# DeltaNet with a multiplicative FFN on one core: corner products of the inverses on four parts of the array, and a new order of all steps

## The chip, the cores and the metric

The kernel runs on one core of a Trainium2 chip. The metric is the device time of one execution in microseconds (us). The profile is one further execution, taken by the hardware profiler; its span is that from the first to the last instruction. In its views PE is TensorE's matmul, PEld its weight load, DVE VectorE, ACT ScalarE, POOL GpSimd and SP SyncE; a q behind a name (SPq) is the engine's queue of instructions, where it issues DMAs. L473 is line 473 of the kernel.

## What is computed

A delta-rule attention over 4 batches, 8 heads, 768 steps and head size 48 feeds a feed-forward block of 3072 tokens, model width 384 and inner width 1024, all in fp32:

```python
k_n = k / (np.linalg.norm(k, axis=-1, keepdims=True) + 1e-06)
for t in range(S):
    kt, vt, bt = (k_n[:, :, t], v[:, :, t], beta[:, :, t, None])
    y[:, :, t] = np.einsum('bhd,bhde->bhe', q[:, :, t], state)
    v_old = np.einsum('bhde,bhd->bhe', state, kt)
    state = state + bt[:, :, :, None] * np.einsum('bhd,bhe->bhde', kt, vt - v_old)
...
a = x @ w1
b = x @ w2
h = a * b @ w3
return (h @ w_out).astype(np.float32)
```

## The kernel before

**Chunks and inverses.** The sequence is cut into 12 chunks of 64 steps (`C`), taken for all 32 pairs of batch and head at once: partitions 0 to 63 hold batches 0 and 1, partitions 64 to 127 batches 2 and 3 (`z` in the code). Within a chunk the recurrence needs the inverse of a triangular 64x64 matrix per pair. `scores` multiplies keys with keys and queries (`KQ`, L360 and L366) and leaves the triangular matrices in `U` and the query scores in `PT`. The inverse is made of 32x32 blocks. `to_blocks` (L408) writes the diagonal blocks of two chunks to DRAM (`Ud`), so that they come back with one block per partition (`Ub`, L420). `inverse` (the 31 steps of L434 and L439 on VectorE) inverts all of them; for the first two pairs of chunks it works in a two-bank PSUM buffer that it holds for that time. The result goes through DRAM (`Vd`, L447), and `from_blocks` (L452) puts the inverted blocks on the diagonal of `TT`, with four DMAs per chunk. `corner` then makes the off-diagonal block in two products per pair: VectorE transposes the upper blocks into `T11` (L464); the block of `U` beside the diagonal times `T11` (L473, 32 small matmuls) goes from quarter 2z of the partitions to quarter 2z+1; ScalarE copies it (L480); times the lower diagonal block (L487, 32 more) it comes back to quarter 2z; ScalarE writes it, negated, into `TT` (L494). Each such matmul has 32 rows, 32 weight columns and 32 moving columns, and its results go to the single-bank buffer `ps_t`.

**The recurrence and its output.** `chain` carries the state: state times keys (S,KQ), subtracted from v into `R`; `R` times `TT` into `X`; `X` times keys into the next state `S` (all L517, 32 matmuls each on 64-row parts of the array). `outputs` (L618) adds state times queries and `X` times `PT`; ScalarE copies it into `xT` (L639), and after every second chunk six DMAs (L650) bring 16 rows of each head group to where the FFN wants them.

**The FFN.** Weights come in pieces: a DMA into one of five `raw` buffers (L663), three ScalarE operations (L671 to L673), one on VectorE (L675) and two on GpSimd (L677, L678) make fp32 of what the inputs hold. `transpose_w3` (L713) and `fold` (L722) multiply w3 with w_out once, into `w34`. For every 128 steps of all four batches `ab` (L742) makes x @ w1 and x @ w2 in eight parts, with their elementwise product (L756), and `o` (L762) multiplies it with `w34`, copies it (L768) and writes it out (L771). These are full 128x128 matmuls of 384 or 512 columns; below they are called dense.

**Order.** Every part of the work is a Python generator that stops at each `yield`. `ORDER` names the part whose next step is written down; a letter for the kind and a number for the chunk or pair of chunks (K, Q, d: keys and queries by features; k, q, v, p: loads; g, N: norms; s: scores; u: to_blocks; V: inverse; e: corner; c: chain; y: outputs; P: a weight piece; t, f: fold; a, o: FFN). `in_text_order` then ties each engine to exactly that order:

```python
for name in ORDER.split():
    step(name)
in_text_order()
```

**PSUM and shared buffers.** `two_banks()` gives `psW` buffers of two banks in turn, two of them; `bank()` single banks of `psF`, three of them; `psT` is one bank. `in_turn` hands out named buffers one after the other, so that the n-th use waits for the end of the one that had the buffer before.

Of the kernel before, what the change touches and what calls it, by code (L numbers as in the profile page):

```python
# [37 lines left out]
P7 k0 g0 q0 V0 K0 g0 g0 k1 K0 K0 P7 P7 P7 K0 K0 Q0 Q0 Q0 Q0 Q0 g0 g0 g0 g0 K1 P0 P0 P0 P0 g0  # L38
P3 K1 K1 K1 P3 P3 s0 g0 beta beta g0 P1 P1 q1 P1 beta N0 s0 K1 Q1 Q1 Q1 P10 P3 s0 s0 Q1 Q1
P1 p2 s0 s0 s0 P10 P10 P10 P6 P6 s1 s1 s1 P11 s1 s1 s1 P6 P6 P13 N0 u0 u1 P11 P11 P12 P2 s1  # L40
d2 d2 t2 t2 P13 P13 N0 P11 P13 V0 V0 P2 P2 P23 V0 P12 P12 t5 P12 P2 P22 P23 P4 V0 P22 V0 V0
V0 V0 V0 P22 V0 V0 V0 t5 V0 P23 P4 P4 t3 t3 k3 t4 P22 t4 t14 t14 f2 P23 f1 P4 V0 V0 V0 V0 P5
P5 P5 v0 P20 P20 V0 V0 V0 V0 V0 t15 P5 f2 V0 V0 P21 P21 f1 f2 P20 n0 n0 f7 V0 V0 V0 V0 P21
V0 V0 V0 P15 P15 P15 V0 f1 V0 V0 t15 p3 P14 P14 s0 P20 k2 t12 f7 P17 t12 P14 f7 P21 t13 g1
g1 P15 f6 p2 d2 d2 g1 V0 V0 V0 t7 t13 d3 t7 P17 f6 f6 P14 g1 g1 g1 P18 t6 t6 P18 s2 e0 P17
g1 g1 f3 e0 g1 g1 N1 e0 P16 e0 P18 P16 s2 s2 s2 e1 e1 s2 s2 e0 f3 P16 e0 c0 c0 P9 P19 P19
P19 f3 P9 P9 P17 t9 t9 p3 P18 t10 t10 v1 y0 y0 e1 e1 P16 t8 t8 d3 d3 P8 d3 s3 s3 s3 P9 P8
P26 P26 s3 s3 s3 u2 P24 t1 t1 u3 c0 c0 P19 t11 P8 n1 n1 N1 N1 P24 e1 P25 V1 P26 P26 c1 f5
P24 c1 e1 c1 c1 t11 V1 V1 V1 V1 V1 V1 V1 V1 V1 V1 f5 f5 P8 t0 t0 k4 s1 y1 y1 V1 P31 V1 V1
P25 P25 f4 P24 V1 P30 V1 V1 V1 V1 V1 V1 f0 P25 P30 P31 P30 P32 g2 v2 P31 c1 P31 V1 V1 f0 V1  # L50
V1 f4 P28 f4 P30 P32 P32 P32 P28 f0 V1 V1 V1 V1 V1 y1 a01 p4 P28 a03 a01 k5 a00 a00 V1 V1
a03 P28 p4 a01 d4 V1 V1 V1 g2 g2 a01 c1 g2 g2 g2 g2 V1 V1 P27 P27 P27 P27 a00 a00 P29 a03
a03 V1 g2 d4 d4 P29 P29 P29 d4 e2 e2 a02 a02 a02 a02 g2 c2 e2 e2 P33 P33 a06 g2 N2 s4 a06 n2
n2 c2 e2 s4 e2 s4 a04 a04 c2 c2 P35 P35 P35 e3 P33 P33 a07 P34 P34 P34 P34 c2 c2 y2 a07 a05
p5 p5 d5 d5 d5 s4 s4 u4 s4 v3 P35 a06 y2 e3 e3 d5 a06 s5 s5 s5 s5 s5 s5 u5 a04 a04 a05 a05
a05 n3 n3 c3 c3 N2 N2 e3 e3 e3 a07 c3 a07 o03 V2 V2 V2 p6 V2 V2 V2 V2 o03 v4 o03 c3 y3 y3 V2
V2 V2 V2 V2 V2 V2 V2 V2 V2 V2 V2 c3 n4 k6 g3 V2 V2 V2 V2 o00 o00 y3 o01 o01 o01 a10 a10 a17
a17 g3 g3 a12 V2 v5 V2 V2 V2 p6 a12 a12 V2 V2 V2 V2 o02 V2 V2 V2 c3 c4 e4 e4 e4 a12 e4 a17
a17 o00 d6 d6 o02 o02 g3 n4 c4 e4 e4 a10 a10 c4 k7 g3 a11 c4 c4 c4 a13 a13 a15 a15 a11 y4 n5
e5 e5 e5 e5 a14 c5 a14 p7 d6 d6 p7 d7 g3 d7 d7 g3 g3 g3 e5 a16 y4 n5 c5 g3 s6 N3 s6 s6 d7 s6  # L60
s6 s6 a16 a16 s7 s7 V3 s7 s7 s7 u6 u7 a11 a11 s7 V3 e5 c5 a16 a13 a13 p8 c5 a14 a14 c5 a15
a15 y5 y5 V3 V3 V3 V3 V3 o12 o12 o13 V3 V3 V3 c5 V3 V3 V3 V3 V3 V3 k8 V3 V3 o13 V3 V3 y5 a20
a20 V3 V3 V3 d8 a27 a27 a23 a24 a24 k9 a23 a23 v6 n6 n6 V3 V3 V3 V3 V3 v7 V3 V3 a23 V3 o12
V3 V3 g4 g4 g4 g4 V3 V4 g4 g4 a27 a27 a20 o13 e6 e6 o10 o10 p8 o10 o11 o11 o11 d8 d8 e7 a20
e6 d8 N3 N3 c6 g4 g4 g4 g4 n7 n7 c6 e6 e6 a25 N4 s8 e7 s8 s8 a24 a24 s8 s8 s8 e6 c6 c6 p9 p9
a25 a25 a25 y6 y6 c6 c6 a21 e7 c7 a21 c7 u8 a22 e7 e7 a22 d9 d9 d9 d9 s9 a22 a22 s9 s9 s9 s9
s9 a21 a21 k10 e7 c7 c7 a26 y7 a26 p10 a26 a26 u9 V4 V4 V4 c7 o21 o21 y7 y7 V4 V4 V4 V4 V4
V4 V4 o22 o21 v8 V4 V4 o22 o22 V4 V4 V4 V4 V4 d10 o23 o23 v9 a35 a35 k11 a37 a37 V4 V4 V4 V4
V4 V4 V4 V4 a34 V4 V4 g5 V4 V4 a34 a37 V4 V4 V4 a35 a35 g5 g5 c7 a37 o20 o20 g5 g5 g5 V4 e9
e8 a36 e8 e8 e8 n9 g5 g5 g5 N4 N4 a36 c8 p10 d10 d10 n8 n8 c8 e8 e8 a30 v11 a30 g5 c8 a30 c8  # L70
y8 y8 d10 s10 a34 p11 p11 c8 e9 e9 a30 N5 n11 d11 d11 a34 d11 s10 s10 a32 d11 s11 s11 s11 V5
a32 a31 c8 a31 a31 a31 e9 e9 c9 n9 c9 s11 s11 s11 a36 n11 s10 s10 s10 u10 u11 V5 a32 a32 e9
c9 c9 a33 a36 a33 o23 a33 N5 y9 y9 y9 a33 o33 o33 o33 V5 V5 V5 o20 V5 V5 V5 o32 V5 V5 o32
o32 V5 V5 V5 N5 a40 a40 a40 V5 a43 V5 V5 V5 V5 V5 V5 V5 V5 V5 V5 a40 a41 a41 a41 a43 V5 V5
o31 a44 a44 o31 V5 a41 o30 v10 V5 c9 V5 V5 V5 o30 V5 V5 V5 e10 e10 o31 n10 n10 e10 a42 e10
e10 e10 e11 a42 c9 c10 a46 a46 a46 a46 c10 a42 a42 c10 c10 a47 a47 y10 y10 e11 e11 e11 a43
a43 c10 c10 o30 a45 a45 a45 a45 a47 a47 c11 c11 e11 e11 a44 a44 c11 c11 o40 o40 y11 o40 y11
y11 o42 o42 o42 o43 o43 o43 a57 a57 a57 a57 a56 a56 a52 a52 a53 a53 a50 a50 o41 a50 a52 a52
o41 o41 a50 a56 a56 a51 a51 a55 a53 a55 a53 a54 a54 a54 a54 a55 a55 a51 a51 o53 o53 o53 o51
o51 o51 o52 o52 o50 o50 o50 o52  # L80
# [4 lines left out]
def kernel(  # L85
# [14 lines left out]
    P = 128  # L100
# [19 lines left out]
    psT = ctx.enter_context(tc.tile_pool(name="psT", bufs=1, space=bass.MemoryType.PSUM))  # L120
    psF = ctx.enter_context(tc.tile_pool(name="psF", bufs=3, space=bass.MemoryType.PSUM))
# [23 lines left out]
    def bank(shape):  # L145
        return in_turn(psF, shape, "f", 3, "ps_f")
# [21 lines left out]
    strict = work.tile([P, P], FP32, name="strict", bufs=1)  # L168
# [10 lines left out]
    def padded(name, shape, n):  # L179
        res = []  # L180
        for i in range(n):
            t = persist.tile(shape, FP32, name=f"{name}{i}")
            pool.memset(t[:], 0.0)
            res.append(t)
        return res
# [5 lines left out]
    ktoks, vtoks, KQs, PTs, Us, Xs, Ss = {}, {}, {}, {}, {}, {}, {}  # L191
# [68 lines left out]
    def squares(j):  # L260
        sums[j] = ss = in_turn(small, [P, 2, 2, NR, H], "ss", 1, "ss")
        for cc in range(2):
            kt = ktoks[2 * j + cc]
            for r in range(NR):
                sq = in_turn(work, [P, H, D], "sq", 1, "sq")
                pool.tensor_tensor(out=sq[:], in0=kt[:, r], in1=kt[:, r], op=ALU.mult)  # L266
                yield
                dve.tensor_reduce(out=ss[:, 1, cc, r], in_=sq[:], axis=AX.X, op=ALU.add)  # L268
                yield
        yield from across(ss[:, 1], ss[:, 0])  # L270
# [79 lines left out]

    def scores(m):
        for r in range(NR):
# [18 lines left out]
            if r == 0:  # L371
                Us[m] = in_turn(work, [P, NR, H, C], "U", 2, "U")
            psv = ps[:].rearrange("p e (a j t) -> p a e j t", a=NP, j=2)
            dve.tensor_tensor(
                out=by_parity(Us[m][:, r]), in0=psv[:, :, :, 0, :],
# [27 lines left out]
    def to_blocks(m):  # L403
        j = m // 2
        if m % 2 == 0:
            Uds[j] = in_turn(dram, [P, BS, BS], "Ud", 2, "Ud")
        for x in range(4):
            sync.dma_start(  # L408
                out=Uds[j][:].rearrange(blocks, x=4, r=NR, h=H)[m % 2, x],
                in_=Us[m][quarter(x), :, :, quarter(x % 2)].rearrange("s r h t -> s (r h) t"),  # L410
            )
        yield
# [36 lines left out]

    def from_blocks(m):  # L450
        for x in range(4):
            sync.dma_start(  # L452
                out=TTs[m % 2][quarter(x), :, :, quarter(x % 2)].rearrange("s r h t -> s (r h) t"),
                in_=Vds[m // 2][:].rearrange(blocks, x=4, r=NR, h=H)[m % 2, x],
            )
        yield


    def corner(m):
        yield from from_blocks(m)  # L460
        TT = TTs[m % 2]

        X1 = T11 = in_turn(work, [P, NR, H, BS], "T11", 2, "T11")
        dve.transpose(  # L464
            out=T11[:].rearrange("p r h t -> p (r h) t"),
# [3 lines left out]
        ps = in_turn(psT, [P, NR, H, BS], "t", 1, "ps_t")  # L469
        for r in range(NR):  # L470
            for h in range(H):
                for z in range(2):
                    pe.matmul(  # L473
                        ps[quarter(2 * z + 1), r, h, :], lhsT=Us[m][quarter(2 * z), r, h, BS:C],
                        rhs=T11[quarter(2 * z), r, h, :], start=True, stop=True,
                    )
        yield
        for z in range(2):
            x = quarter(2 * z + 1)
            act.copy(out=X1[x], in_=ps[x])  # L480
        yield
        ps = in_turn(psT, [P, NR, H, BS], "t", 1, "ps_t")
        for r in range(NR):
            for h in range(H):
                for z in range(2):
                    x = quarter(2 * z + 1)
                    pe.matmul(  # L487
                        ps[quarter(2 * z), r, h, :], lhsT=X1[x, r, h, :],
                        rhs=TT[x, r, h, BS:C], start=True, stop=True,
                    )  # L490
        yield
        for z in range(2):
            x = quarter(2 * z)
            act.mul(out=TT[x, :, :, BS:C], in_=ps[x], mul=-1.0)  # L494
# [391 lines left out]
```

## Time and profile before

| | |
|---|---|
| time, median of 3 runs | 611.39 us (611.18 to 611.51) |
| span of the profiled execution | 610.1 us |
| mean granted TensorE clock | 0.991 |
| TensorE busy | 567.9 us |
| dense products: x @ w1, x @ w2, output, fold | 131.1, 131.5, 127.1, 46.8 us busy |
| corner products, first and second | 15.1, 14.6 us busy, 768 rows each |
| scores, both lines | 30.6 and 31.3 us busy |
| ScalarE copies of the first corner product | 24, 577 ns each |

A program matmul shows as two rows in these views, so 24 corner products of 32 matmuls are 1536 rows. A row lasts longer than the step from one row to the next[...]: what a phase costs is read from the start of one phase to the start of the next, in the timeline. A line of the timeline gives the start, the length, engine, line, operation, output and inputs, shapes and the number of rows run together; what stands in brackets is idle time before it. In a line of busy times by stretches there follow, after the stretch and its length, PE, PEld, DVE, ACT and POOL with the number of instructions, then the granted clock, the DMA engines' share and GB/s.

### The profile page before, as it was taken

How to read it: one execution, taken by the hardware profiler on the slowest of the kernel's cores; microseconds unless marked ns; L12 is line 12 of the kernel's file. 1: busy time of each engine (PE TensorE's matmuls, PEld its weight loads, DVE VectorE, ACT ScalarE, POOL GpSimd, SP SyncE). 2: the span in 40 equal slices, each digit the busy share in tenths (PEclk: the TensorE clock that was granted, in tenths of full speed). 3: DMA queues.
4: the chain of work that ended last, by engine and by line, in shares of the span. 5: the costliest groups of instructions: out<-in, count | busy, mean ns of one | idle time of the engine just before them, and what ended most of it. 6: DMA issues, size and time to landing. Idle time of an engine off the chain costs nothing.

```text
span 610.1 us, 17982 instructions
## 1 busy us (share of the span) xinstructions
PE 567.9 (93%) x7804; PEld 333.7 (55%) x7804; DVE 322.0 (53%) x752; ACT 183.2 (30%) x373; POOL 145.3 (24%) x150
## 2 busy tenths in 40 slices
PE   3736988999899999999999999999999999999997
PEld 2724667644565655655466655465564655644454
DVE  1569875697665955557946449556386123100110
ACT  2776667654530212402111302122121212211100
POOL 6489866575242101100130000112001000000000
PEclk9999997899999999999999999999999999999999
DMA  9668887867755255253356324551321300000001
GB/s 216 163 207 195 195 176 168 193 118 155 158 77 105 67 116 85 30 94 72 62 119 87 55 55 96 101 74 23 57 81 26 97 2 2 24 30 13 1 13 39
DMA packets 202223, 55.67 MB, mean 91 GB/s; under 512 B 192352, under 2 KB 195424, under 8 KB 202144
## 3 DMA queue, kind: packets, MB, share of 16 engines
q1 hardware_dynamic: 197952, 53.74, 42.0%
q10 hardware_dynamic: 4192, 0.79, 0.9%
q8 instruction: 61, 1.00, 0.7%
q14 instruction: 18, 0.15, 0.1%
HBM read 42.30 MB, written 11.01 MB: 87 GB/s over the span
## 4 chain that ended last, share of the span: by engine, by line
PE 83%; SPq 5%; DMA 4%; ACT 3%; DVE 2%; issue 1%; POOL 1%; ACTq 0%; POOLq 0%; DVEq 0%
PE ps_f L742 38%; PE ps_f L762 20%; PE ps_f L722 5%; PE ps_w L517 5%; PE ps_w L618 4%; PE ps_t L473 2%; PE ps_w L366 2%; PE ps_t L487 2%; PE ps_w L360 2%; SPq L226 2%; PE ps_f L713 1%; SPq L663 1%; DMA X<-in_q_dram 1%; DMA raw<-in_moe_w_out_dram 1%; DMA ktok<-in_k_dram 1%
## 5 line engine op out<-in xcount | busy, mean ns | idle before, releaser
L742 PE MATMUL ps_f<-xT,w1s 128*128 128x512 f32 x288 | 131.1, 600 | 1.5 <-DMA xT<-xT 1.5
L742 PE MATMUL ps_f<-xT,w2s 128*128 128x512 f32 x288 | 131.5, 600 | 0.5 <-DVE ab L756 0.5
L762 PE MATMUL ps_f<-w,ab 128*128 128x384 f32 x384 | 127.1, 488 | 0.1
L756 DVE TENSOR_TENSOR ab<-a,ps_f 128x512 f32<-128x512 f32 x48 | 32.6, 683 | 136.5 <-PE ps_f L742 135.6
L762 PEld LDWEIGHTS ps_f<-w,ab 128*128 128x128 f32 x384 | 72.3, 190 | 51.5 <-issue 3.3
L742 PEld LDWEIGHTS ps_f<-xT,w2s 128*128 128x128 f32 x288 | 53.0, 190 | 61.2 <-issue 57.6
L742 PEld LDWEIGHTS ps_f<-xT,w1s 128*128 128x128 f32 x288 | 53.0, 190 | 60.4 <-issue 55.0
L751 ACT COPY a<-ps_f 128x512 f32<-128x512 f32 x48 | 27.7, 585 | 148.3 <-PE ps_f L742 116.5
L266 POOL TENSOR_TENSOR sq<-ktok 128x384 f32<-128x384 f32 x24 | 20.2, 844 | 147.7 <-DVE ss L268 82.1
L768 ACT COPY osb<-ps_f 128x384 f32<-128x384 f32 x24 | 11.5, 479 | 126.0 <-PE ps_f L762 97.0
L503 POOL TENSOR_TENSOR vtok<-vtok,n 128x384 f32<-128x384 f32 x24 | 20.2, 858 | 117.0 <-DMA vtok<-in_v_dram 103.9
L439 DVE TENSOR_TENSOR Vb<-Vb,tb 128x31 f32<-128x31 f32 (+15 forms) x124 | 45.2, 364 | 4.3
L722 PE MATMUL ps_f<-w2s,w3T 128*128 128x384 f32 x128 | 46.8, 518 | 0.1
L434 DVE TENSOR_TENSOR tb<-Vb,Ub 128x31 f32<-128x31 f32 (+15 forms) x124 | 43.9, 354 | 4.6 <-DMA Ub<-Ud 0.7
L639 ACT COPY xT<-ps_w 48x256 f32<-48x256 f32 x96 | 30.5, 366 | 48.4 <-PE ps_w L618 31.9
L722 PEld LDWEIGHTS ps_f<-w2s,w3T 128*128 128x128 f32 x128 | 24.9, 202 | 16.3 <-issue 2.7
L366 PE MATMUL ps_w<-KQ 48*64 48x64 f32 x768 | 31.3, 241 | 0.0
L360 PE MATMUL ps_w<-KQ 48*64 48x128 f32 x384 | 30.6, 307 | 0.7 <-ACT PT L386 0.7
L360 PEld LDWEIGHTS ps_w<-KQ 48*64 48x64 f32 x384 | 25.3, 154 | 8.6 <-issue 6.6
L713 PE MATMUL ps_f<-ident,w 128*128 128x128 f32 x64 | 12.6, 335 | 17.9 <-POOL w L678 17.9
L366 PEld LDWEIGHTS ps_w<-KQ 48*64 48x64 f32 x768 | 28.7, 154 | 0.3 <-issue 0.2
L581 DVE TENSOR_TENSOR S<-S,ps_w 48x768 f32<-48x768 f32 x20 | 19.0, 950 | 9.7 <-PE ps_w L517 9.5
(94 smaller groups left out, 642.4 us busy)
## 6 DMA issues: line engine op xcount, KB each, us to landing
raw<-in_moe_w_dram SPq DMA_DIRECT2D x16, 512.0 KB, 5.5
vtok<-in_v_dram SPq DMA_DIRECT2D x24, 192.0 KB, 4.0
raw<-in_moe_w_dram SPq DMA_DIRECT2D x24, 192.0 KB, 4.2
out_dram<-osb SPq DMA_DIRECT2D x24, 192.0 KB, 2.0
ktok<-in_k_dram SPq DMA_DIRECT2D x44, 96.0 KB, 3.4
raw<-in_moe_w_out_dram SPq DMA_DIRECT2D x8, 384.0 KB, 4.8
Ud<-U SPq DMA_DIRECT2D x48, 64.0 KB, 2.0
Ub<-Ud SPq DMA_DIRECT2D x6, 512.0 KB, 3.4
```

The costliest lines, as they stand in the source:

```text
L360: pe.matmul(ps[half(z), 0, n : n + 128], lhsT=x[:, 0, :], rhs=x.rearrange("p j t -> p (j t)"), start=True, stop=True,)
L366: pe.matmul(ps[half(z ^ j), 1, n + C * j : n + C * j + C], lhsT=x[:, 0, :], rhs=x[:, j, :], start=True, stop=True,)
L434: dve.tensor_tensor(out=tv, in0=V[:, 0 : s + 1, s : s + 1].to_broadcast([P, s + 1, n]), in1=U[:, s, s + 1 : BS].unsqueeze(1).to_broadcast( ...
L439: dve.tensor_tensor(out=o, in0=o, in1=tv, op=ALU.subtract)
L517: pe.matmul(out(ps, r, h, z), lhsT=lhs(r, h, z), rhs=rhs(r, h, z), start=True, stop=True,)
L618: i = pe.matmul(region(h, z, r), lhsT=lhs, rhs=rhs, start=part[n] not in part[:n], stop=part[n] not in part[n + 1 :],)
L639: act.copy(out=xT[f, p:NP:2, b : b + NR, cc, :].rearrange("p a r t -> p r a t"), in_=pyv[f, z, b : b + NR],)
L722: pe.matmul(ps[:, 0:DM], lhsT=w3Ts[jc, kc // 4][:, kc % 4 * P : kc % 4 * P + P], rhs=wo[:, kc], start=(kc == 0), stop=(kc == KF - 1),)
L742: pe.matmul(ps[:], lhsT=w[:, m, js], rhs=x[:, m].rearrange("p b c t -> p (b c t)"), start=(m == 0), stop=(m == KM - 1),)
L751: act.copy(out=a[:], in_=ps[:])
L756: dve.tensor_tensor(out=t[:], in0=a[:], in1=ps[:], op=ALU.mult)
L762: pe.matmul(ps[:, 0:DM], lhsT=abs_[u, jc][:, b * P : (b + 1) * P], rhs=w34[:, jc, :], start=(jc == 0), stop=(jc == KF - 1),)
```

## The change

- **Corner products.** Both products use 64-row, 64-column parts of the array: rows 64z to 64z+32 (33 rows, the last of them zeros in one operand), 33 weight columns, 33 output partitions. The output goes to the half z of even heads and to the other half of odd heads, so that all four parts are used; the two parities go to the two banks of a `psW` buffer. The second product, of heads that crossed over, takes them back. It reads the lower diagonal block from a new tile `T22`, which holds odd heads on the other half.
- **`from_blocks`** loads `T22` with four more DMAs per chunk (eight in place of four).
- **Buffers.** `U` and `T11` are persistent tiles with 8 more columns that are set to zero; `T11` is one buffer in place of two; `T22` is two. `psT` is gone and `psF` has four banks. `strict` and the squares `sq` share the buffers of the output copies (`o`).
- **`ORDER`** is written anew from the first step to the last: the same steps but in another sequence on all engines. Weight pieces begin with P0 in place of P7; corners, chains and scores stand at other places among the dense products.

```diff
-P7 k0 g0 q0 V0 K0 g0 g0 k1 K0 K0 P7 P7 P7 K0 K0 Q0 Q0 Q0 Q0 Q0 g0 g0 g0 g0 K1 P0 P0 P0 P0 g0
...
-o51 o51 o52 o52 o50 o50 o50 o52
+k0 g0 K0 q0 P0 k1 P3 P0 g0 P0 K1 P7 g0 K0 K0 beta K0 K1 K0 g0 P3 g0 P10 K1 P1 P7 P0 K1 Q0 K1 P3
...
+o51
...
-    psT = ctx.enter_context(tc.tile_pool(name="psT", bufs=1, space=bass.MemoryType.PSUM))
-    psF = ctx.enter_context(tc.tile_pool(name="psF", bufs=3, space=bass.MemoryType.PSUM))
+    psF = ctx.enter_context(tc.tile_pool(name="psF", bufs=4, space=bass.MemoryType.PSUM))
...
+    Us = padded("U", [P, NR * H * C + 8], 2, NR * H * C)
...
+    T11s = padded("T11", [P, NR * H * BS + 8], 1, NR * H * BS)
+    T22s = padded("T22", [P, NR, H, BS], 2)
+
     def from_blocks(m):
+        V = Vds[m // 2][:].rearrange(blocks, x=4, r=NR, h=H)[m % 2]
...
+        T22 = T22s[m % 2]
+        for z in range(2):
+            for e in range(2):
+                sync.dma_start(
+                    out=T22[quarter(2 * (z ^ e))].rearrange("s r (a e) t -> s e (r a) t", e=2)[:, e],
+                    in_=V[2 * z + 1].rearrange("s (g e) t -> s e g t", e=2)[:, e],
+                )
         yield
...
-        ps = in_turn(psT, [P, NR, H, BS], "t", 1, "ps_t")
...
-                    pe.matmul(
-                        ps[quarter(2 * z + 1), r, h, :], lhsT=Us[m][quarter(2 * z), r, h, BS:C],
-                        rhs=T11[quarter(2 * z), r, h, :], start=True, stop=True,
...
+        def rows(z):
+            return slice(C * z, C * z + BS + 1)
+
+        def products(lhs, rhs):
+            ps = two_banks()
+            for n in range(NR * H):
                 for z in range(2):
+                    i, o = lhs(n, z)
                     pe.matmul(
+                        ps[rows(o), n % 2, n // 2 * BS : n // 2 * BS + BS],
+                        lhsT=i, rhs=rhs(n, z), start=True, stop=True,
                     )
...
+        ps = products(
+            lambda n, z: (U[rows(z), C * n + BS : C * n + C + 1], z ^ n % 2),
+            lambda n, z: T11[rows(z), BS * n : BS * n + BS],
+        )
...
+        ps = products(
+            lambda n, z: (T11[rows(z ^ n % 2), BS * n : BS * n + BS + 1], z),
+            lambda n, z: T22[rows(z ^ n % 2), n // H, n % H, :],
+        )
```

## The prediction

> **What bounds the kernel now.** I read the page first (busy shares, the 40 slices, the chain of waits), then busy time by stretches, then TensorE's timeline with the start of every phase.
>
> ```profile
> PE 567.9 (93%) x7804; PEld 333.7 (55%) x7804; DVE 322.0 (53%) x752; ACT 183.2 (30%) x373; POOL 145.3 (24%) x150
> PE   3736988999899999999999999999999999999997
> PEclk9999997899999999999999999999999999999999
> DMA  9668887867755255253356324551321300000001
> ```
>
> ```profile
> 90.00:105.00 15.00, 11.94 (x354) 10.23 (x352) 8.21 (x14) 13.10 (x27) 10.14 (x10) 0.77 0.79 165
> 300.00:400.00 100.00, 99.77 (x1381) 57.19 (x1382) 58.87 (x144) 17.79 (x40) 10.78 (x14) 1.00 0.43 81
> 130.83:606.25 475.42, 471.72 (x6176) 263.76 (x6176) 236.84 (x542) 99.51 (x214) 54.75 (x60) 1.00 0.33 65
> ```
>
> The reader is to see two kernels in one. From 130.83 us, where the first product with w1 starts, to the last matmul at 606.25, TensorE is busy 471.72 of 475.42 us. There, time is TensorE's own pitch and nothing else. Before 130.83 it is idle for some 34 of the 42.2 us that it idles in all, and near 92 to 110 us its clock is cut too. What holds that stretch is the latency of the first inverse and one queue: SyncE issues DMAs almost without a gap from 63 us on, and the copies into `xT` that the first w1 product waits for leave last.
>
> ```profile
> 122.87 3.93 SPq L663 DMA_DIRECT2D raw<-in_moe_w_dram  x4
> 126.90 3.75 SPq L650 DMA_DIRECT2D xT<-xT  x6
> 130.83 7.96 PE L742 MATMUL ps_f<-xT,w1s 128*128 128x512 f32 x18 [1.48 <-DMA xT<-xT]
> ```
>
> For the dense stretch the starts of neighbours on TensorE's timeline give the price of each phase:
>
> ```profile
> 235.72 1.15 PE L517 MATMUL ps_w<-R,TT 64*64 64x48 f32 x64
> 236.80 2.84 PE L742 MATMUL ps_f<-xT,w1s 128*128 128x512 f32 x6
> 239.57 0.94 PE L517 MATMUL ps_w<-X,ktok 64*48 64x48 f32 x64
> 240.44 5.42 PE L742 MATMUL ps_f<-xT,w1s 128*128 128x512 f32 x12
> ...
> 425.96 1.20 PE L487 MATMUL ps_t<-TT,T 32*32 32x32 f32 x64
> 427.10 1.15 PE L517 MATMUL ps_w<-S,KQ 48*64 48x48 f32 x64
> 428.06 0.29 PE L360 MATMUL ps_w<-KQ 48*64 48x128 f32 x2
> ...
> 455.00 2.74 PE L742 MATMUL ps_f<-xT,w1s 128*128 128x512 f32 x6
> 457.57 2.74 PE L742 MATMUL ps_f<-xT,w2s 128*128 128x512 f32 x6
> ```
>
> A row is half a program matmul (32 in the code, x64 here). Six dense rows take 2.57 us among dense rows (455.00 to 457.57) but 2.77 between two small phases (236.80 to 239.57). A 64-row L517 phase takes 1.08 before a dense group (235.72 to 236.80) and 0.96 before another small phase of the same tile size (427.10 to 428.06). A corner product takes 1.14 (425.96 to 427.10), 1.13 elsewhere, whatever stands beside it, and the L517 phase before a corner takes 1.08 (226.84 to 227.92), as before a dense group.
>
> [...] The trace has L517's 64 rows on X and ktok in 0.71 us net, 11.1 ns a row or 22 ns a program matmul[...] the added copies move 128-byte runs, like most packets here (192352 of 202223 under 512 B).
>
> **The change, part by part.**
> *Price of a mode change.* An L517 phase loses 0.12 on leaving. It loses 0.04 on entering: X,ktok takes 0.87 between dense groups, 0.83 (335.07 to 335.90) with a small phase ahead. Its two dense neighbours lose 0.20 together. That is 0.36 for an island, 0.18 a change; I use 0.17, which closes the sum. Net phases of the stretch: 96 dense groups at 2.57 are 246.7, 24 output groups at 5.21 (278.95 to 289.38 is two) 125.0, 20 L517 products at 0.92 and 9 at 0.71 24.8, 16 score halves at 0.93 14.9, 10 output attentions at 2.1 21.0, 8 crossings 0.8, 20 corner products at 1.13 - 0.16 = 0.97 19.4: 452.6. In the built program's order I count 113 changes of mode there, corners included: 19.2. Sum 471.8, measured 471.7. So the price list holds.
>
> *Corner products.* Net time of a row, times the number of array parts in use, is 57.5 ns for 64 columns (0.92/64 x 4), 44.4 for 48, 30.3 for the old corner's 32 columns on two parts. That is columns x 0.83 + about 4.3. The new one loads 33 columns on four parts: 31.8/4 x 64 = 0.51 us. The trace shows no row faster than 11.1 ns: 0.71. [...] I take 0.60, between the formula and the fastest row shown[...]. Saving 0.37 each[...]: 7.4 us over the 20 in the dense stretch. The four earlier ones lie beside waits and I count them at nothing.
>
> *Order and mode.* The new corners have the size of their small neighbours, and the new order has fewer islands (42 against 47 after the first w1 product). Changes of mode fall from 113 to 84 there: 29 x 0.17 = 4.9 us. Before it they fall from 27 to 20, again beside waits.
>
> *New waits.* Three times the new order puts only an L517 phase and a crossing (1.1 us) between a corner's two products. In the profile the way through ScalarE's two copies (0.577 each) took 1.34, from 83.18 to 84.52: 0.25 each, 0.8 in all. Behind the waiting matmul stands all of TensorE. Corner results now take the two-bank buffers; between a use and the next but one there stands nearly always a dense group of 2.57 us, longer than the 1.2 to 1.9 us of copies: nothing. The fourth single bank only loosens waits. The two sums of squares now share tiles with the output copies, on engines with 30% and 24% load: nothing. The single `T11` makes VectorE's transpose wait for the corner before it, which the order places at least a phase ahead: nothing.
>
> *Startup.* The pads are 1.2 us more on GpSimd (two memsets like qperm's 0.95 at half size, three tiny), ahead of its first work. From writing back the first inverse to the `xT` copies, SyncE gets 73 issues in place of 67, eight of them for `T22`: +6 x 0.484 (median of the TT loads) = 2.9 us. The odd chunk's TT loads also go behind three weight loads. Against that, TensorE's order has fold groups between the corner's products and behind the second chain, so the idle time and cut clock at 92 to 110 us (some 7 us) may shrink. But the `xT` copies were SyncE-bound, not TensorE-bound: 120.4 us had the last ScalarE copy, 126.9 the first issue. I take 0, with -4 (half of the idle and clock loss returned) and +5 (2.9 of issues and 2 of weight loads ahead of TT) as ends.
>
> *Later DMA issues.* 40 more at 0.484, 19 us, on a SyncE that waits 141 us for output copies alone: hidden by those waits.
>
> Sum against the profile's own span: 610.1 - 7.4 - 4.9 + 0.8 = 598.6. The three timed runs stand 1.3 above the span (611.39), so 599.9; forecast **600**.
>
> **Rivals.**
> *The startup gives too* (594): formula price 0.51 (another -1.8), startup -4: 598.6 - 5.8 + 1.3. For it: 7 us of idle and slow clock lie open at 92 to 110. Against it: SyncE's queue sets the first w1 product.
> *The corners hardly gain* (607):[...] with the four parts not overlapping (31.8/2 x 64 = 1.02 us, no gain at all; the change then doesn't do what it says), 4.9 from mode changes[...] remain, less 0.8 of waits, with 0 to 4 us of startup loss. For it: no row at 8 ns in the trace. Against it: three shapes lie on one line.
> *Slower* (613): SyncE. The odd chunk's TT loads wait behind three weight loads, each of which waits for GpSimd to free a raw buffer. In the profile such loads went on to 84.5 us, against 78.4 for TT. TensorE's queue stands still behind that chunk's first corner product, and everything up to the first w1 product shifts. If TT comes 10 us later than I think, and the gap costs another 5 us of halved clock as at 92 to 110 us, the first w1 product comes at 146: 599.9 + 15 = 615, less 2 from the 0.51 price. It decides from 11 us of delay. Against it: TensorE wants that product only near 92 us, and TT lands by 90 on the old pace.
>
> **Chances.** Forecast's own case (596 to 604) 0.55; startup gives too 0.18; corners hardly gain 0.16; slower 0.11. The range 590 to 607 leaves out the slower case and the top of the third. A change under 0.2% (1.2 us) can't be told from none: same gets 0.03, cut from the third and fourth cases; faster 0.87, slower 0.10.
>
> **What would show it.** Right: corner rows in 0.5 to 0.7 us; 64-row phases at 0.96 beside corners; busy TensorE from the first w1 product on near 459 us; that product between 127 and 136. Wrong: corners near 1.0; idle TensorE over 5 us in the dense stretch; a first w1 product outside 124 to 140.

## The result, and the profile after

The kernel after took **605.24 us** (median of 4 runs, 601.56 to 608.43), beside 611.45 (611.18 to 614.23) for the kernel before on the same chip: a ratio of 0.9878, with a 95% interval of 0.9832 to 0.9924. That is 1.2% faster, and 5.2 us slower than the forecast of 600.0. The profiled execution has a span of 602.6 us, where the profile of before has 610.1. Medians, ranges and ratios below leave out executions over 1.5% above the fastest of their kernel: three with 64 rows ahead, two with the old corner, one of the last run, and four of the kernel before.

First the page: busy shares, and TensorE and its clock in the 40 slices.

```profile
PE 553.2 (92%) x7804; PEld 321.5 (53%) x7804; DVE 323.1 (54%) x752; ACT 183.1 (30%) x373; POOL 147.0 (24%) x155
PE   3706996999899999999999999999999999999997
PEclk9955996899999999999999999999999999999999
```

Then busy time by stretches (TensorE, its weight loads, VectorE, ScalarE, GpSimd, then clock, DMA share and GB/s), for two of the stretches that were shown of before:

```profile
300.00:400.00 100.00, 98.61 (x1430) 55.51 (x1429) 61.51 (x145) 19.32 (x42) 10.73 (x14) 1.00 0.43 81
131.64:599.22 467.58, 460.76 (x6184) 254.95 (x6176) 241.39 (x547) 98.83 (x214) 53.12 (x59) 1.00 0.37 70
```

The kernel still falls into two parts. The first w1 product starts at 131.64 us (before: 130.83), so the startup has neither given nor taken. All of the gain lies in the dense stretch: 467.58 us in place of 475.42. TensorE is busy 460.76 us of it in place of 471.72, 11.0 less. But it is idle 6.8 us in place of 3.7, and the stretch from 300 to 400 us, 99.77 busy before, is now 98.61. So something new stops TensorE there.

TensorE's timeline (start, duration, line, operation, rows; in brackets the idle time ahead and what ended it) shows a corner, and one of these stops:

```profile
177.72 0.75 PE L492 MATMUL ps_w<-T,U 33*33 33x32 f32 x64 [0.60 <-DVE PT L391]
178.39 2.84 PE L770 MATMUL ps_f<-xT,w2s 128*128 128x512 f32 x6
...
437.55 0.70 PE L545 MATMUL ps_w<-X,ktok 64*48 64x48 f32 x43
439.44 0.47 PE L545 MATMUL ps_w<-X,ktok 64*48 64x48 f32 x21 [1.19 <-issue]
439.85 1.56 PE L790 MATMUL ps_f<-w,ab 128*128 128x384 f32 x4
```

A corner product ahead of a dense group takes 0.67 us (177.72 to 178.39; 0.68 at 154.86), where it took 1.13. Ahead of another small phase it takes 0.61:

```profile
248.79 0.76 PE L492 MATMUL ps_w<-T,U 33*33 33x32 f32 x64
249.40 1.15 PE L545 MATMUL ps_w<-S,KQ 48*64 48x48 f32 x64
```

The stop at 439.44 lies in the middle of a 64-row phase: 43 rows run, nothing for 1.19 us, then the other 21. All of its operands were used by rows before it. "issue" means that the profile shows nothing to wait for. TensorE's waits over the whole span, by what ended them (total, times, longest), list four such groups:

```profile
PE ps_w L367 <- issue: 2.6, 1, 2.6
PE ps_w L545 <- issue: 2.3, 2, 1.2
PE ps_w L492 <- issue: 2.2, 1, 2.2
PE ps_w L646 <- issue: 2.0, 2, 1.1
```

These are 9.1 us in six stops; the kernel before has one, `PE ps_t L487 <- issue` of 0.7 us. Three of the six (0.84 at 331.02, 1.19 at 439.44, 1.12 at 499.57) are in the dense stretch, 3.15 us together.

What happens 2.4 us earlier gives a cause to test. The page's list of DMA queues (packets, MB, share) has a queue of the kind `instruction`, and the DMA view of 437.0 to 438.1 us shows one packet of it, at 437.08:

```profile
q8 instruction: 61, 1.00, 0.7%
...
q8 instruction: 1, 0.02, 5.5%
```

61 packets of 1.00 MB in all are 16 KB each. TensorE has 7804 rows (matmul records), each with a weight load of its own: 15608 instructions, or 256 to a packet. So one packet would be 128 rows; with the 139 semaphore waits and drains that the trace has in the same queue it is some 127. In this trace each of the six stops ends 2.2 to 2.8 us after a packet starts (437.08 to 439.44 is 2.36).

### The profile page after: what moved, and what is told of

The parts are those of the page before. It is cut to its first block, busy times and chain, and to the rows that moved or that the text cites. A ratio compares the mean times of both kernels' runs of the same rounds, so it can differ in the third digit from the quotient of the medians.

```text
span 602.6 us, 18069 instructions
## 1 busy us (share of the span) xinstructions
PE 553.2 (92%) x7804; PEld 321.5 (53%) x7804; DVE 323.1 (54%) x752; ACT 183.1 (30%) x373; POOL 147.0 (24%) x155
## 4 chain that ended last, share of the span: by engine, by line
PE 77%; DMA 7%; SPq 6%; DVE 4%; issue 3%; ACT 2%; ACTq 0%; POOL 0%; DVEq 0%; POOLq 0%
PE ps_f L770 39%; PE ps_f L790 21%; PE ps_w L545 5%; PE ps_w L646 4%; DMA raw<-in_moe_w_dram 3%; SPq L224 3%; PE ps_f L750 3%; PE ps_w L492 2%; DMA TT<-Vd 2%; PE ps_w L361 1%; PE ps_w L367 1%; DVE ps_w L439 1%; SPq L456 1%; DMA ktok<-in_k_dram 1%; DVE tb L434 1%
## 5 line engine op out<-in xcount | busy, mean ns | idle before, releaser
L770 PE MATMUL ps_f<-xT,w1s 128*128 128x512 f32 x288 | 129.2, 596 | 0.0
L434 DVE TENSOR_TENSOR tb<-Vb,Ub 128x31 f32<-128x31 f32 (+15 forms) x124 | 45.8, 369 | 13.3 <-DMA Ub<-Ud 9.6
L373 DVE TENSOR_TENSOR U<-ps_w,wt 128x512 f32<-128x512 f32 x24 | 16.5, 689 | 34.4 <-PE ps_w L367 34.4
L367 PE MATMUL ps_w<-KQ 48*64 48x64 f32 x768 | 29.5, 230 | 2.8 <-issue 2.6
L741 PE MATMUL ps_f<-ident,w 128*128 128x128 f32 x64 | 12.9, 357 | 18.2 <-POOL w L706 18.2
L361 PE MATMUL ps_w<-KQ 48*64 48x128 f32 x384 | 28.3, 289 | 0.4 <-ACT PT L385 0.4
L367 PEld LDWEIGHTS ps_w<-KQ 48*64 48x64 f32 x768 | 26.7, 144 | 3.1 <-issue 2.8
L361 PEld LDWEIGHTS ps_w<-KQ 48*64 48x64 f32 x384 | 22.7, 142 | 6.2 <-issue 5.6
```

Source lines behind the costliest of these rows:

```text
L361: pe.matmul(ps[half(z), 0, n : n + 128], lhsT=x[:, 0, :], rhs=x.rearrange("p j t -> p (j t)"), start=True, stop=True,)
L367: pe.matmul(ps[half(z ^ j), 1, n + C * j : n + C * j + C], lhsT=x[:, 0, :], rhs=x[:, j, :], start=True, stop=True,)
L434: dve.tensor_tensor(out=tv, in0=V[:, 0 : s + 1, s : s + 1].to_broadcast([P, s + 1, n]), in1=U[:, s, s + 1 : BS].unsqueeze(1).to_broadcast( ...
L770: pe.matmul(ps[:], lhsT=w[:, m, js], rhs=x[:, m].rearrange("p b c t -> p (b c t)"), start=(m == 0), stop=(m == KM - 1),)
```

## The experiments

The kernels ran in three groups of four, each group on one chip beside the kernel before (medians 612.43, 612.69 and 612.75 us). The letters of the theories are explained in each expectation; the main one, **A**, is that TensorE runs out of instructions where one fetched piece holds small phases only.

**The kernel after once more** (no edit).

> The changed kernel itself, to have it beside the others and to see a second trace. Theory A (TensorE runs out of instructions: the six stops without a wait that the profile of the changed kernel shows, 9.1 us, are fetches of 16 KB of instructions that come too late): the stops stand at the same rows again, their lengths differ by some tenths, the median lies between 601 and 608. Rival B (a wait that the profile does not show, on another engine): stops at other places or none.

605.34 us (602.49 to 606.71), ratio 0.9897 [0.9845, 0.9948]. The stops stand inside the same phases, at the same rows: in the dense stretch at row 4663 of TensorE's program (0.30 us, after 0.85), 6568 (0.98, after 1.19) and 7203 (1.11, after 1.12). They belong to places in the program, not to accidents of one run.

**Half a piece of rows ahead of everything.** 32 dummy products, 64 rows, 128 instructions:

```diff
+    dummy = bank([P, 512])
+    for _ in range(32):
+        pe.matmul(
+            dummy[half(0), 0:C], lhsT=ident[half(0), half(0)], rhs=ident[half(0), half(0)],
+            start=True, stop=True,
+        )
     running = {}
```

> 32 matmuls of 64x64 that nobody reads are put ahead of everything on TensorE, which is idle there: 64 rows, 128 instructions, half of a 16 KB block. Theory A: the stops without a wait go away from the places where they were (331.0, 439.4 and 499.6 us in the profile of the changed kernel, the 55th, 40th and 35th row counted modulo 128) and come up 64 rows away, where that falls into small phases; time within 4 us of the changed kernel's either way. Rival B: they stay in the same phases, and the time stays within 1 us.

612.18 us (607.33 to 615.78; 613.29 with all twelve runs), ratio 1.0005 [0.9968, 1.0042]. The whole gain is gone, though no work in the dense stretch differs; that is 7 us more than after, where A allowed 4. All three stops have left their places, and new ones stand at 206.77 (1.09), 237.47 (1.80), 328.79 (1.69), 368.62 (1.27) and elsewhere. (Its profile is of one of the executions left out, 617.0.) The first w1 product comes at 131.46, so the loss isn't in the startup. The moved stops fit A, the size of the loss doesn't. This doesn't exclude that the dummies cost something by themselves; the next run does.

**A whole piece, a quarter, three quarters**: the same edit with 64, 16 and 48 dummies (128, 32 and 96 rows).

> The kernel after with 64 dummy 64x64 products ahead of everything: 128 matmul rows, 256 instructions, which is exactly one of the 16 KB fetches of instructions; twice as many dummies as in the run with 64 rows (613.3 us). Theory A (TensorE runs out of instructions where one fetched piece holds small phases only): the pieces have their borders at the same rows of the program as in the kernel after, so the stops come back to the rows at which that kernel has them (there at 331, 439 and 499 us), and the time to 604 to 608 us. Theory D (the dummies themselves, or a program that is longer, cost the 8 us): 613 us or more, up to 620.

609.74 us (607.21 to 614.90), ratio 0.9960 [0.9938, 0.9981]. With twice as many dummies the kernel is 2.4 us faster than with 64 rows, and the stops are back where the kernel after has them. TensorE's timeline of this run, at the place shown above:

```profile
442.43 0.70 PE L545 MATMUL ps_w<-X,ktok 64*48 64x48 f32 x43
444.32 0.47 PE L545 MATMUL ps_w<-X,ktok 64*48 64x48 f32 x21 [1.19 <-issue]
```

It is the same phase, cut after the same 43 rows, for the same 1.19 us. The other two are back too, at rows 4663 + 128 and 7203 + 128. So 128 rows of dummies, 256 instructions, bring the places back, as A says and as dummies that cost by themselves can't give. The time itself is 1.7 us over what A allowed and 4.4 over the kernel after: the first w1 product is 2.0 us later (133.62), the stop at row 7203 is 1.7 in place of 1.1, and two more waits on issue come, 1.40 us at 136.11 and 0.83 at 175.17. The first of these, two rows behind the first w1 product, lies at no border of a piece; what it waits for isn't shown.

> As before with 48 dummies, 96 rows, 192 instructions: the borders lie at three quarters of a piece. Theory A: the stops sit at other rows than with 0, 64 and 128 rows, and time less stops is the same; the time lies anywhere in 601 to 613 us, by what work the borders fall into, and follows the sum of the stops and of the lower clock behind them. Theory D: 613 to 617.

**601.51 us** (600.00 to 606.25), ratio 0.9835 [0.9789, 0.9881]: the best median of the study. The phase shown above runs through (64 rows from 434.79 to 435.63), and the dense stretch has 1.8 us of stops.

> As before with 16 dummies, 32 rows, 64 instructions: the borders lie at a quarter of a piece. Theory A: other rows again, 601 to 613 us by the sum of the stops. Theory D (dummies cost in proportion): about 607 to 609 us with the stops where the kernel after has them.

617.75 us (613.55 to 619.43), ratio 1.0061 [1.0017, 1.0105]: slower than the kernel before, and 4.8 over A's upper end. Its dense stretch shows how a stop can cost more than its length. TensorE's timeline, then busy time by stretches, where the clock is the third number from the end:

```profile
237.13 0.68 PE L492 MATMUL ps_w<-T,T 33*33 33x32 f32 x55
239.16 0.27 PE L492 MATMUL ps_w<-T,T 33*33 33x32 f32 x9 [1.35 <-issue]
239.36 3.61 PE L770 MATMUL ps_f<-xT,w1s 128*128 128x512 f32 x4
```

```profile
237.00:239.00 2.00, 0.70 (x57) 0.58 (x56) 1.21 (x5) 0.08 (x1) 0.00 (x0) 1.00 0.61 67
239.00:241.00 2.00, 1.84 (x11) 0.83 (x11) 0.00 (x0) 1.18 (x2) 0.00 (x0) 0.64 0.77 120
241.00:243.00 2.00, 2.00 (x4) 0.91 (x3) 0.00 (x0) 0.00 (x0) 0.00 (x0) 0.50 0.48 79
```

After 1.35 us without work the granted clock is 0.50, and four dense rows have a duration of 3.61 us, where the six at 178.39 in the kernel after have 2.84. Stops in this run's dense stretch add up to 8.4 us, 5.2 more than after. The clock is at 0.50 for 3.4 us three times (from 181.5, 239.6 and 331.7 us), half of which, 5.1 us, I count as lost. Waits on other engines are 1.7 longer. Together that is 12.0 of the 12.2 us by which its dense stretch is longer.

**The kernel before, with the same dummies** (32, 64 and 96 rows).

> The kernel before with 16 dummy 64x64 products (32 rows, 64 instructions) ahead of everything, as in the run of the kernel after with 32 rows, which was 12 us slower than without. Theory A1 (the kernel before suffers as much from where the borders of the fetched pieces fall, and stands at a lucky place): stops in the dense stretch where it has none after 156 us, 614 to 622 us. Theory A2 (its order is robust, since its corners were twice as long and dense groups stand between its small phases): 611 to 613 us at each of the three places, no stop over 1 us in the dense stretch.

> The kernel before with 32 dummies (64 rows). A1: 612 to 622 us, at other rows than with 32; A2: 611 to 613 us.

> The kernel before with 48 dummies (96 rows), where the kernel after came to 601.5. A1: 612 to 622 us; A2: 611 to 613 us. Over the four places the mean of the kernel after is 609.5 us (605.3, 617.8, 613.3, 601.5): under A1 the mean of the kernel before is 3 to 8 us above that, under A2 1 to 3 us.

613.63 us (609.87 to 617.68), 625.09 (621.33 to 625.47) and 619.64 (617.43 to 625.24), ratios 1.0016 [0.9996, 1.0036], 1.0171 [1.0121, 1.0222] and 1.0107 [1.0070, 1.0145]. With 64 rows ahead the old kernel stops just as the new one does; its timeline:

```profile
203.52 0.80 PE L517 MATMUL ps_w<-X,ktok 64*48 64x48 f32 x52
206.11 0.38 PE L517 MATMUL ps_w<-X,ktok 64*48 64x48 f32 x12 [1.79 <-issue]
```

Theory A2, a robust old order, falls at 64 and 96 rows; at 64 rows the time is even 3 us over A1's upper end. At 32 rows the result is near what A2 expected (no stop, and 0.6 us over its upper end), and A1's 614 to 622 was too high. So the kernel before, as it was, stood at a lucky place. All placements together ("dense stretch" is from the start of the first w1 product to that of the last matmul, in the profiled execution; "stops" are the waits on issue in it; "rest" is the dense stretch without the stops and without half of the time that it spent at a clock of 0.50):

| rows ahead | before: us | dense stretch, stops, rest | after: us | dense stretch, stops, rest |
|---|---|---|---|---|
| 0 | 612.8 | 474.9, 0, 474.9 | 605.3 | 467.1, 3.2, 463.9 |
| 32 | 613.6 | 475.1, 0, 475.1 | 617.8 | 479.3, 8.4, 465.8 |
| 64 | 625.1 | 489.6, 8.1, 476.4 | 612.2 | 479.9, 7.5, 463.9 |
| 96 | 619.6 | 482.3, 5.1, 477.2 | 601.5 | 465.6, 1.8, 463.8 |
| mean | 617.8 | 480.5, 3.3, 475.9 | 609.2 | 473.0, 5.2, 464.4 |

Three of the profiles have the clock at 0.50 in the dense stretch: before with 64 rows for 10.2 us, after with 32 for 10.2 and with 64 for 17.1 (in the execution of 617.0 us). Where it isn't cut, the dense stretch grows by 1.1 to 1.4 us for 1 us of stop; where it is, by 1.8 to 2.5. The placement moves the time by 16 us in the kernel after and by 12 in the kernel before, both more than the change does. Over the four placements the change is worth 8.6 us, 1.4%, a little over A1's 3 to 8. Four of some 127 placements are a small sample: the differences are -7.5, +4.2, -12.9 and -18.1. What the table calls rest is steadier: that of the changed kernel is 9.3 to 13.4 us shorter at every placement, 11.5 in the mean. So the change itself gains at all four, and the stops with the cut clock behind them decide how much of it is seen.

The places of the stops say the same. Counted from the first row of the program, dummies included, the rows of all 20 stops over 0.25 us in the four traces of the kernel after leave 91 to 93 when divided by 127: 4410 has one with 32 rows ahead and with 64, 4663 and 6568 with none and with 32. So the borders of the pieces stand still, and the dummies move the work across them.

**The old corner in the new order.** The corner's products on two parts with 32 x 32 tiles, all else as after:

```diff
-                        ps[rows(o), n % 2, n // 2 * BS : n // 2 * BS + BS],
-                        lhsT=i, rhs=rhs(n, z), start=True, stop=True,
+                        ps[quarter(2 * z + o), BS * n : BS * n + BS],
+                        lhsT=lhs(n, z), rhs=rhs(n, z), start=True, stop=True,
```

> The changed kernel with the corner products as they were before (32 rows and columns, two parts of the array, X1 in the other quarter), all buffers, loads and the new order as changed. Theory A: 24 products at 0.97 us net in place of 0.52, 9.0 us in the dense stretch, and 19 changes of tiling mode more at 0.17 us, 3.2: 12 us more there, less up to 3 us of stops that the slower phases avoid: 9 to 12 us over the changed kernel, that is 611 to 617, so that the new order alone gains nothing over the kernel before. Rival C (the gain is the order's, the corners' is lost to the stops): 2 to 5 us over the changed kernel.

613.11 us (609.73 to 615.31), ratio 1.0013 [0.9995, 1.0031]; 7.8 us over the kernel after in the same group. So the new order by itself gives nothing that can be seen in the time at this placement, and the new corner gives the gain. Busy time of its dense stretch:

```profile
131.18:609.90 478.72, 472.08 (x6182) 265.07 (x6176) 241.03 (x548) 98.93 (x214) 53.41 (x59) 1.00 0.36 69
```

TensorE is busy 472.08 us there, 0.4 more than in the old order (471.72) and 11.3 more than with the new corner (460.76). But from 156.2 to 159.6 us its clock is at 0.50, which by the same count costs 1.7. Reckoned as in the table, its stops are 3.4 us and its rest is 473.4: 1.5 under the old order with the old corner, 9.5 over the new order with the new one. So some 1.5 us are the order's and 9.5 the corner's, at this one placement. The reverse, the new corner in the old order, wasn't run.

**Without the T22 loads.** The four DMAs of each chunk are left out, so the corner's second product reads the zeros that `T22` was set to, and the off-diagonal blocks of the inverses are left out.

> The changed kernel without the 48 loads of T22, which stays zero, so that the off-diagonal blocks of the inverses are left out. Theory A: in the first 90 us SyncE is given back the 8.9 us that its first eight loads took there, and the first product with w1 (131.6 us in the profile) comes 2 to 5 us sooner; later nothing: 2 to 5 us less than the changed kernel. Rival D (these loads are hidden): within 1 us of it.

601.06 us (600.85 to 604.91), ratio 0.9848 [0.9797, 0.9899]: 4.3 less than after. Its profile (of the longest execution) has the first w1 product at 129.39, 2.3 us earlier, after 4.2 us of waiting for its `xT` copies; but the unchanged kernel's second trace has it at 129.84 too. SyncE's timeline of the kernel after shows how long the loads held that queue:

```profile
73.81 3.19 SPq L463 DMA_DIRECT2D T<-Vd  x4
...
82.18 5.74 SPq L463 DMA_DIRECT2D T<-Vd  x4
```

The first eight loads hold SyncE for 8.9 us, 0.80 and 1.43 us each. That is not their own price: the median of all 48 is 0.45, and four loads of keys at 59.29 took 1.31 each. What slows the queue in the startup isn't shown.

**The T22 loads on ScalarE's queue**, throughout:

```diff
-                sync.dma_start(
+                act.dma_start(
                     out=T22[quarter(2 * (z ^ e))].rearrange("s r (a e) t -> s e (r a) t", e=2)[:, e],
```

> The kernel after with the new T22 loads issued on ScalarE's queue in place of SyncE's. If SyncE's time is what the startup waits for (the kernel without these loads took 4 us less): SyncE gets 8.9 us back in 70 to 90 us, the first w1 product starts 2 to 4 us earlier than at 131.6 us, and the time is 601 to 604 us. If ScalarE, which would wait for the bounce through DRAM before it issues them, holds up the work behind it as much: 604 to 608. If the loads were hidden and the 4 us of that run are a matter of where the stops fell: no change, 605 us.

615.79 us (613.64 to 617.96), ratio 1.0052 [1.0029, 1.0075]: 10 us slower than after, which none of the three expectations allowed. The first w1 product came as early as the first of them said, and the dense stretch lost more than that: it is 15 us longer. TensorE's timeline, and below it waits from 131 to 330 us by what ended them:

```profile
129.12 1.10 PE L770 MATMUL ps_f<-xT,w1s 128*128 128x512 f32 x2 [1.33 <-DMA xT<-xT]
```

```profile
ACT osb L796 <- DMA TT<-Vd: 15.0, 1, 15.0
PE ps_f L790 <- ACT osb L796: 3.3, 1, 3.3
```

The first w1 product comes 2.5 us earlier (0.7 earlier than in the second trace of the kernel after). But an output copy on ScalarE once waited 15.0 us, until a load of the inverse's blocks from DRAM had landed. The copy needs nothing of these blocks; the T22 loads ahead of it in ScalarE's queue read the same DRAM tile, and ScalarE's queue stood 13.5 us at a semaphore of theirs. TensorE waited 3.3 us for the copy. Two waits ahead of corners, 2.75 us at 153.79 and 4.86 at 183.06, came on top; the trace names VectorE as their releaser, so that they hang together with ScalarE's queue is argued and not shown.

**Both together**: 48 dummies, and only the first two chunks' loads on ScalarE.

> The kernel after with 48 dummies (96 rows) and, for the first two chunks alone, the T22 loads on ScalarE's queue; later chunks keep them on SyncE's. With them on ScalarE's queue throughout, the first w1 product came at 129.1 us and not 131.6, and the dense stretch lost 15 us to waits for what ScalarE evicts late; with 96 rows alone it was 601.5 us with that product at 128.8. If the two gains add: first w1 product 126 to 127.5, 599 to 600.5 us. If both only remove the same wait at the startup: 601 to 602.5. If ScalarE's wait in the startup holds up the folds: 603 or more.

603.86 us (599.13 to 606.11), ratio 0.9817 [0.9766, 0.9868]. In its profile the first w1 product is at 133.81, not earlier but 5 us later than with 96 rows alone; the dense stretch, 466.7 us, is 1.1 longer than there. The third expectation named such a time, but its reason isn't shown. The median is inside the other's range and its own range is 7 us, so this is inconclusive, and gives no reason to move the loads. Whether the T22 loads cost the 4.3 us stays open: with them, at different placements, the first w1 product came anywhere between 128.8 and 133.8.

## Why the prediction was right, and where it was wrong

The forecast of faster was right, and the time lies in the range of 590 to 607; the size was 5.2 us off. That the time fell into the range owes something to luck: with 32 or 64 rows ahead the same change would have taken 617.8 or 612.2 us, outside the range and no faster than the 612 of the kernel before as it was. Against the spans: the sum said 598.6, and the profile has 602.6.

- **The corner price** came out better than forecast. Start to start, the 20 corner products of the dense stretch take 13.4 us and not 22.6: -9.2, or 0.46 each. Ahead of a dense group one takes 0.67 to 0.69; ahead of another small phase, with no change of mode behind it (a step between dense tiles, 64-row parts of the array and 32-row parts), 0.61 (248.79 to 249.40). That is the 0.60 that I chose, not the formula's 0.51; inside that product the rows start 9.0 ns apart in the mean, 0.57 us from the first to the last, between the two. The old one took 1.13 everywhere, so a part of the 0.46 belongs to the next term. 0.67 us for 32 program matmuls is 21 ns each, and 10.5 for each row as the trace counts it, where the fastest rows of before took 11.1 net.
- **The changes of mode**, -4.9, were forecast too high. Their price, 0.17 us, was my estimate from the starts of neighbours (among them 1.08 us for an L517 phase ahead of a dense group, 0.96 ahead of one of its own size); what TensorE does at a change isn't shown. With the corners' 7.4 that is 12.3, and TensorE's busy time fell by 11.0. The 9.2 of the corners contain some changes of mode; outside them at most 1.8 came. Start to start, the dense groups gave 1.2 (five islands fewer, at the 0.20 of two dense neighbours, are 1.0), chains and scores 1.0, and output attentions and crossings took 0.6 more. The run with the old corner in the new order has, counted as in the prediction, 103 changes in place of 113, which at 0.17 should save 1.7; with the 1.7 lost to the clock taken off, its busy time fell by 1.3. So the price is nearly borne out for these ten. It was read off an island between dense groups and applied to all 29. Whether the other 19, between corners and small phases, or the corner's own price made the forecast 1.3 too high, the runs don't separate.
- **The three new waits**, +0.8: nothing of them is seen. Idle time without the stops is 6.82 - 3.15 = 3.67 us, and was 3.70.
- **The startup**, 0: +0.8, well inside its bounds of -4 to +5. Its working was less good than its result: the first eight loads hold SyncE for 8.9 us, where eight at the working's 0.484 are 3.9 (2.9 for six more issues in all). The median was a fair price for a load, 0.45 over all 48; in the crowded startup it doesn't hold. That the first w1 product moved by 0.8 only shows that other parts gave this back; which ones isn't shown.
- **Missing**: the stops, +3.15, the largest single error. No term stood for them, and nothing in the profile of before drew the eye: a single wait of 0.7 us, and a queue with 0.7% of the DMA time. But the trace held the two numbers that mattered, 256 instructions to a packet and small phases of 11 to 19 ns a row (0.71 us for 64, 0.93 for 48). The prediction's own mark for being wrong, more than 5 us of idle TensorE in the dense stretch, came true (6.8).

The sum with what was measured: 610.1 - 9.2 - 1.8 + 3.15 + 0.8, and 0.4 less behind the last matmul, gives 602.65; the span is 602.6. The 1.8 is what the measured busy time leaves, so this close is no test. It rests on one profile of each kernel; the four timed runs of the kernel after spread over 7 us and the 28 to 31 runs of the kernel before in a group over 6 to 8, and why is not settled.

Of the rivals, *the corners hardly gain* falls with the 0.67 us, *slower by SyncE* with the first w1 product at 131.64, and *the startup gives too* with the same. None had the slower outcome that the runs did find: at another placement of the same program, 32 rows on, the changed kernel is slower than before.

## What to carry to other kernels

In this kernel, where TensorE runs long rows of tiny matmuls, its instructions were a resource: by my estimate a piece of some 127 rows needed about 3.2 us, and six stops took 9.1 us. In such a kernel see how long each run of that many rows takes, and put dense groups between small phases by that count, not by phases. Before you judge a change of 1% in such a kernel, measure both kernels with a few dummy rows ahead, since here the placement alone was worth 12 to 16 us; and take stops and cut clock off the profile's spans, which showed the change's own gain at every placement. A price that was read off one kind of neighbours must be tried on the others before it is multiplied.

## What the runs showed of the hardware

- **Feeding TensorE.** A packet of instructions comes on for every 127 rows or so (61 packets for 7804 rows, 15608 instructions with their weight loads, and the 139 others). In all 20 stops counted above, rows go on 2.2 to 2.8 us after a packet starts (in one stop of the kernel before, 3.2). In 16 of the 20 the packet starts 0.5 to 1.4 us after the first row of the piece before; in the kernel after the three pieces ahead of a stop take 3.3, 3.4 and 3.0 us from first row to first row, the stop included. So I estimate that a piece needs about 3.2 us. From this I took the starts of the kernel after without its stops, and called a stop wherever a piece takes less than 3.2 us. Over 0, 32, 64 and 96 rows ahead it names the places of 18 of the 20 stops of over 0.25 us that the dense stretches show. It also names 9 that did not come. So the rule finds the risk; what lets a packet start earlier in those 9 cases stays open.
- **The clock behind a stop.** Idle times of TensorE of 1.35, 1.91 and 1.98 us (the kernel after with 32 rows), and of 1.88 and even 0.81 (the kernel before with 64), were followed by 3.4 or 6.8 us at a clock of 0.50; others of up to 2.21 us (the kernel before with 32 rows, at 180.04) by none. So an idle time under 2 us, beside small phases, can be enough here, and a longer one can pass. What decides it isn't shown.
- **Issues of DMAs.** An issue of the T22 loads took 0.45 us in the median of 48, but 0.80 to 1.43 for the first eight, in a crowded SyncE queue; on ScalarE's queue the same eight took 0.46 to 0.49.
